# Gate steps of a mixture of experts with operands in a PSUM bank, transposes of two tiles in one bank, scatter places copied out of the rows, and own banks for the last two tiles

## The chip, the cores and the metric

The kernel runs on one core of a Trainium2 chip. The metric is the device time of one execution in microseconds (us). TensorE is called PE here, VectorE DVE, ScalarE ACT, GpSimd POOL and SyncE SP, as in the profile. SBUF is the on-chip memory that all engines read. PSUM is the memory that PE writes its results into; it has banks of 128 x 512 fp32 values ("bank" below always means one of these).

## The reference

Three stages, each feeding the next, in fp32:

```
x = scan(x, a, B, C)                 # state space scan, 4 x 8 x 768 x 32, chunks of 32
x = x.reshape(3072, 256)
h = x @ w_in                         # FFN, 256 -> 2048, rational activation
g = (a0 + a1 h + a2 h^2 + a3 h^3) / (1 + |b0||h| + |b1|h^2 + 1e-6)
x = g @ w_out                        # 2048 -> 256
# mixture of 8 experts, each token to its best one
xn = x / (norm(x) + 1e-6);  en = emb / (norm(emb) + 1e-6)
logits = xn @ en.T / tau
idx = argmax(logits);  p = softmax(logits)     # exp, sum + 1e-9, divide
out[n] = p[n, idx[n]] * (relu(x[n] @ w1[idx[n]]) @ w2[idx[n]])   # 256 -> 1024 -> 256
```

## The kernel before

The whole program is recorded as a list of operations, and a planner (class `Plan`) writes it out in an order of its own. Each operation gives its engine (or a choice of engines), an assumed length, and a number `at`. At each moment a free engine takes, of the operations whose inputs are ready and whose buffers are free, the one with the smallest `at`. Buffers come from groups with a name ("tag") and a fixed count; a group hands them out strictly in the order of their first use. Each engine then runs its own list in that fixed order, and waits where an input isn't there yet.

**The mixture of experts.** A token's row has 265 numbers: 256 values, 8 logits, and its place in the output as an integer. `route` (L778) computes logits of 128 tokens at a time (`tk`, PE L799 and L801; copied to `row` by ACT L804), finds each token's expert, and POOL scatters the rows into an expert's region of `xs` in DRAM. Then passes run over experts sorted by how many tokens they hold.

- Three *first passes* (`first_pass`) take 256 tokens of each of the three largest experts, with fp32 weights `fa`, `fb`; they are interleaved with the end of the FFN, so PE has work while routing finishes. Their rows are `fg`, their first matmuls `fh`, their activations `fr`, their second matmuls `fy`.
- The *later passes* (`run_pass`) take 256 more tokens of each of these three, 384 of each of the four smallest (`e4` to `e7`), and last 512 of expert 3 in two parts. These use weights split into a high and a low half, loaded by `weights` (L935): SP's queue loads `ra` or `rb` (L946), ACT rounds to the high half `eah`/`ebh` (L947), and DVE or POOL subtracts to get the low half `eal`/`ebl` (L950). The four buffers of tag "raw" that receive `ra` and `rb` also hold the rows `fg` of the first passes.

A later pass consists of: `tokens` (L955), which loads rows `g`, transposes them on PE (`t`, L969), and splits the transpose into `xh` (ACT L972) and `xl` (DVE L975); `gate` (L981), which computes the softmax weight `gt` of each token from its own row by some 11 small DVE steps on 128 x 2 to 128 x 32 numbers (L994 to L1008: `s`, `sq`, `rc`, `mx`, `ex`) with ACT steps between (L990, L995, L996, L1005); eight times `hidden` (L1011), with matmuls `eh` (L1023), `hh` on ACT (L1025), `hl` on DVE (L1026) and second matmuls `y` (L1032); and `deliver` (L1038), which scales `y` by `gt` into `yo` (ACT or DVE, L1046 or L1048) and scatters it to the output from POOL (L1052, an indirect DMA whose places are read from the rows `g`).

After all routing, `beyond` (L1176) counts the tokens that fit in no pass: one small matmul `ck` and nine or so small DVE steps.

The FFN's lines are L738 to L755 (`h`, `v`, `u`, `p`, `gh`, `gl`, `acc`); L776 writes its result `x2T`.

Of the kernel before, what the change touches and what calls it, by code (L numbers as in the profile page):

```python
# [275 lines left out]
def ssm_ffn_moe_kernel(  # L276
# [153 lines left out]
    tri, ones = keep([P, P], BF16, "tri"), keep([P, P], BF16, "ones")  # L430
    io, tok, cw8, ke, kmin = keep([P, NE], I32, "io"), keep([P, NCH], I32, "tok"), keep([P, NE], F32, "cw8"), keep([P, NE], BF16, "ke"), keep([P, NE], F32, "kmin")
# [1050 lines left out]
```

## Time and profile before

| | |
|---|---|
| time, median of 3 runs | 608.58 us (608.17 to 608.62) |
| the profiled execution, time | 609.72 us |
| its span in the trace | 607.9 us, granted clock 0.980 in the mean |
| PE busy | 555.0 us, 91% |
| DVE busy | 478.7 us, 79% |
| ACT busy | 467.1 us, 77% |
| POOL busy | 249.7 us, 41% |

The span is the time from the first to the last event of the trace; an execution's time has 1.8 us around it. The chain of waits that ends last goes through PE for 59% of the span. The FFN ends at about 418 us in the span, routing and first passes fill the time to about 457, and the later passes run from there to 595.3; the last 12.6 us deliver the last tiles.

### The profile page before, as it was taken

To read this page: it belongs to the slowest core of one execution; us is meant where nothing else is said; L and a number is where in the kernel's file an instruction comes from. 1 tells how busy PE (TensorE), PEld (TensorE's weight loads), DVE (VectorE), ACT (ScalarE), POOL (GpSimd) and SP (SyncE) were. 2 spreads that over 40 slices of the span, in tenths; PEclk is the share of its full clock that TensorE was granted. 3 is DMA by queue.
4 is the path that set the end of the run, shared out by engine and by line. 5 is a ranking of instruction groups with operands and counts; after the bars stand their busy time and mean duration, and the time that the engine had idled before them with its cause. 6 is when DMAs were issued, how large, how long until landed. Compare 5 with 4: busy or idle time off the path is not lost.

```text
span 607.9 us, 10415 instructions
## 1 busy us (share of the span) xinstructions
PE 555.0 (91%) x3429; PEld 430.0 (71%) x3429; DVE 478.7 (79%) x989; ACT 467.1 (77%) x941; POOL 249.7 (41%) x233
## 2 busy tenths in 40 slices
PE   1667989999999999999999999899998979999991
PEld 0244657776667666767676787677888979999991
DVE  7997899989888798899997889884456667767430
ACT  6898989999998899989997998893256667557330
POOL 2573334446444444454445434433433543222111
PEclk9997999999999999999999999999999989999996
DMA  7960515113102120110010001681266855544000
GB/s 245 390 206 18 160 30 160 45 55 97 45 0 84 51 61 19 54 62 18 2 46 27 1 2 54 219 286 36 89 193 174 238 154 177 173 142 153 18 23 14
DMA packets 47919, 61.08 MB, mean 100 GB/s; under 512 B 4135, under 2 KB 37776, under 8 KB 47856
## 3 DMA queue, kind: packets, MB, share of 16 engines
q1 hardware_dynamic: 45360, 53.92, 29.0%
q0 software_dynamic: 2496, 6.41, 2.9%
q8 instruction: 29, 0.48, 0.4%
q14 instruction: 34, 0.28, 0.1%
HBM read 46.11 MB, written 14.72 MB: 100 GB/s over the span
## 4 chain that ended last, share of the span: by engine, by line
PE 59%; issue 8%; DMA 7%; DVE 7%; ACT 4%; POOL 3%; SPq 1%; another core or an unknown queue 0%; POOLq 0%; ACTq 0%
PE h L738 19%; PE acc L764 19%; PE eh L1023 4%; PE y L1032 4%; PE c L666 3%; DMA g<-xs 2%; PE y L706 2%; PE y L712 2%; DMA ra<-in_w 2%; POOL out_dram L1052 1%; PE tk L801 1%; PE fy L1119 1%; DMA out_dram<-yo,g 1%; DMA fa<-in_w 1%; DVE gh L752 1%
## 5 line engine op out<-in xcount | busy, mean ns | idle before, releaser
L755 POOL TENSOR_TENSOR gl<-p,v 128x512 fp32r<-128x512 f32 x96 | 127.4, 1329 | 176.0 <-DVE p L754 76.1
L738 PE MATMUL h<-x1h,wiw 128*128 128x512 f32 x384 | 142.0, 413 | 7.5 <-DVE p L754 5.2
L764 PE MATMUL acc<-gh,wow 128*128 128x512 f32 x384 | 112.0, 413 | 0.0
L738 PEld LDWEIGHTS h<-x1h,wiw 128*128 128x128 f32 x384 | 73.5, 192 | 34.0 <-issue 7.6
L764 PEld LDWEIGHTS acc<-gh,wow 128*128 128x128 f32 x384 | 68.0, 188 | 29.6 <-issue 15.9
L752 DVE SCALAR_TENSOR_TENSOR gh<-h,as,v 128x512 fp32r<-128x512 f32 x96 | 71.7, 747 | 14.1 <-ACT v L750 13.5
L753 DVE SCALAR_TENSOR_TENSOR u<-u,lq,gh 128x512 f32<-128x512 f32 x96 | 78.9, 822 | 0.8
L747 DVE SCALAR_TENSOR_TENSOR h<-p,sl,h 128x512 f32<-128x512 f32 x96 | 71.9, 749 | 6.7 <-ACT v L744 6.4
L738 PE MATMUL h<-x1l,wiw 128*128 128x512 f32 x192 | 76.8, 400 | 0.0
L743 ACT ACTIVATE p<-h,kk 128x512 f32<-128x512 f32 x96 | 65.3, 680 | 11.8 <-POOL gl L755 6.1
L754 DVE SCALAR_TENSOR_TENSOR p<-h,as,u 128x512 f32<-128x512 f32 x96 | 71.6, 745 | 3.0 <-DVE bw L651 0.2
L745 ACT ACTIVATE u<-v,qb 128x512 f32<-128x512 f32 x96 | 69.5, 724 | 1.5
L749 ACT ACTIVATE v<-u,lq 128x512 f32<-128x512 f32 x96 | 69.4, 722 | 1.6
L750 ACT ACTIVATE v<-v 128x512 f32<-128x512 f32 x96 | 60.4, 630 | 1.0
L764 PE MATMUL acc<-gl,wow 128*128 128x512 f32 x192 | 60.6, 396 | 0.1
L744 ACT ACTIVATE v<-h 128x512 f32<-128x512 f32 x96 | 56.9, 593 | 2.5 <-POOL gl L755 2.5
L1026 DVE SCALAR_TENSOR_TENSOR hl<-eh,hh 128x256 fp32r<-128x256 f32 (+1 forms) x72 | 34.2, 479 | 27.3 <-ACT hh L1025 26.8
L1025 ACT ACTIVATE hh<-eh 128x256 fp32r<-128x256 f32 (+1 forms) x72 | 30.5, 425 | 28.2 <-PE eh L1023 24.4
L1052 POOL DMA_INDIRECT out_dram<-yo,g x22 | 23.8, 1080 | 67.8 <-DVE yo L1048 34.6
L1032 PE MATMUL y<-ebh,hh 128*128 128x256 f32 x176 | 51.2, 291 | 0.3 <-ACT hh L1025 0.3
L1032 PE MATMUL y<-ebh,hl 128*128 128x256 f32 x176 | 50.5, 287 | 0.2 <-DVE hl L1026 0.2
L1032 PE MATMUL y<-ebl,hh 128*128 128x256 f32 x176 | 49.8, 283 | 0.0
(238 smaller groups left out, 1143.1 us busy)
## 6 DMA issues: line engine op xcount, KB each, us to landing
ra<-in_w SPq DMA_DIRECT2D x32, 256.0 KB
rb<-in_w SPq DMA_DIRECT2D x32, 256.0 KB
xb<-in_xb SPq DMA_DIRECT2D x12, 384.0 KB
xs<-empty SPq DMA_DIRECT2D x8, 530.0 KB
wiwr<-in_w_in SPq DMA_DIRECT2D x8, 512.0 KB
wowr<-in_w_out SPq DMA_DIRECT2D x8, 512.0 KB
xrow<-row SPq DMA_DIRECT2D x6, 530.0 KB
bc<-in_bct SPq DMA_DIRECT2D x12, 256.0 KB
```

The costliest lines, as they stand in the source:

```text
L738: T.matmul(out=h.t, lhsT=part(wiw[g_], z)[:, k, fs], rhs=xx[:, k, :], start=(k == 0 and e == 0), stop=(k == 1 and e == 2))
L743: op("ACT", act(512, 1), s, lambda: A.activation(out=pp.t, in_=h.t, func=AF.Square, bias=kk.t), r=[h, kk], w=[pp])
L745: op("ACT", acts(512) + 0.06, s + 0.3, lambda: A.activation(out=uu.t, in_=vv.t, func=AF.Square, bias=qb.t), r=[vv, qb], w=[uu])
L747: op("DVE", dve(512, 1), s + 0.8, lambda: stt(out=h.t, in0=pp.t, scalar=sl.t, in1=h.t, op0=ALU.add, op1=ALU.mult), r=[h, pp, sl], w=[h])
L749: op("ACT", acts(512) + 0.09, s + 0.9, lambda: A.activation(out=vv.t, in_=uu.t, func=AF.Ln, bias=lq.t), r=[uu, lq], w=[vv])
L750: op("ACT", acts(512), s + 1.0, lambda: A.activation(out=vv.t, in_=vv.t, func=AF.Exp, scale=-1.0), r=[vv], w=[vv])
L752: op("DVE", dve(512, 1), s + 1.5, lambda: stt(out=gh.t, in0=h.t, scalar=as_.t, in1=vv.t, op0=ALU.add, op1=ALU.mult), r=[h, as_, vv], w=[gh])
L753: op("DVE", dve(512, 1), s + 1.6, lambda: stt(out=uu.t, in0=uu.t, scalar=lq.t, in1=gh.t.bitcast(F32), op0=ALU.add, op1=ALU.mult), r=[uu, l ...
L754: op("DVE", dve(512, 1), s + 1.7, lambda: stt(out=pp.t, in0=h.t, scalar=as_.t, in1=uu.t, op0=ALU.add, op1=ALU.subtract), r=[h, as_, uu], w ...
L755: op("POOL", pool2(512), s + 2.1, lambda: G.tensor_tensor(out=gl.t, in0=pp.t, in1=vv.t, op=ALU.mult), r=[pp, vv], w=[gl])
L764: T.matmul(out=acc[dh].t, lhsT=part(wow[g_], z)[:, i % 2, dh * P:(dh + 1) * P], rhs=x.t, skip_group_check=True, start=(i == 0 and e == 0), ...
L1032: T.matmul(out=y[t // 2][:, t % 2 * DM:(t % 2 + 1) * DM], lhsT=hx[:, o], rhs=wb[w][:, f % 2, :], start=(f == 0 and i == 0 and t % 2 == 0), ...
```

## The change

1. **Gate's steps with operands in a bank.** All gates but that of the first small pass take a bank (`gp`, of the four with tag "h" that `eh` and `fh` use too) and put `rc`, the later `sq`, `mx` and `ex` there; none of the steps then has two inputs in SBUF. One DVE step (the clamp, L994) is dropped: ACT's Ln gets the constant 1e-36 as its bias from a tile `tiny`, set once on POOL.
2. **Two tiles' transposes to a bank.** `tokens` transposes two tiles into one bank, and one ACT copy and one DVE subtraction of 512 columns do what two of 256 did.
3. **Places copied out of the rows.** POOL copies the places into `ix` (later passes) or `fix` (first passes); the scatter reads them there, and so the rows `g` and `fg` are no longer held until it.
4. **The last two tiles in own banks** (`apart`). In the last part of the last pass each tile's `y` has a bank and its matmuls are an operation of their own; the first tile's `yo` then depends on its own matmuls alone.

```
+    op("POOL", 0.1, 30.0, lambda: G.memset(tiny.t, 1e-36), w=[tiny])
...
-        for t in range(n):
+        for t in range(0, n, 2):
+            m = min(2, n - t)
...
-            op("PE", 0.218, at - 2 + 0.3 * t, f, r=[g, ident], w=[tr])
-            op("ACT", act(256), sh(at - 2 + 0.3 * t, 0.08, 0), f1, r=[tr], w=[(xh, t)])
-            op("DVE", dve(256), at + -2.0 + 0.3 * t, f2, r=[tr, (xh, t)], w=[(xl, t)])
+            op("PE", 0.218 * m, at - 2 + 0.3 * t, f, r=[g, ident], w=[tr])
+            op("ACT", act(256 * m), at - 2 + 0.3 * t + 0.08, f1, r=[tr], w=xp(xh))
+            op("DVE", dve(256 * m), at - 2.0 + 0.3 * t, f2, r=[tr] + xp(xh), w=xp(xl))
...
+        if bankd:
+            gp = plan.val(ps_h, [P, 512], F32, f"gp{nm}", "h", H_B, True)
+            SN, RC, MX, EX = ((gp, k) for k in range(4))
+            sn, rc, mx3 = ((lambda k=k: gp[:, 32 * k:32 * k + n]) for k in range(3))
+            ex = lambda: gp[:, 96:96 + n * NE].rearrange("p (t e) -> p t e", e=NE)
...
-        dv(0.08, lambda: V.tensor_scalar(out=s2[:, 0:n], in0=s2[:, 0:n], scalar1=1e-36, scalar2=None, op0=ALU.max), [s2], [s2])
...
-        dv(0.1, lambda: V.reciprocal(out=rc[:, 0:n], in_=s[:, 0:n]), [s], [rc])
-        dv(0.08, lambda: V.tensor_tensor(out=rc[:, 0:n], in0=rc[:, 0:n], in1=s2[:, 0:n], op=ALU.mult), [rc, s2], [rc])
-        dv(0.08, lambda: V.tensor_tensor(out=s[:, 0:n], in0=s[:, 0:n], in1=rc[:, 0:n], op=ALU.add), [s, rc], [s])
...
+        dv(0.1, lambda: V.reciprocal(out=rc(), in_=s()), [S], [RC])
+        dv(0.08, lambda: V.tensor_tensor(out=rc(), in0=rc(), in1=s2[:, 0:n], op=ALU.mult), [RC, s2], [RC])
+        dv(0.08, lambda: V.tensor_tensor(out=sn(), in0=s(), in1=rc(), op=ALU.add), [S, RC], [SN])
+        dv(0.08, lambda: V.tensor_scalar(out=sn(), in0=sn(), scalar1=0.5, scalar2=1e-6, op0=ALU.mult, op1=ALU.add), [SN], [SN])
+        dv(0.1, lambda: V.reciprocal(out=rs(), in_=sn()), [SN], [RS])
...
+        for t in range(n):
+            op("PE", 1.4 / 4, sh(at + 0.8, 0.36, 0) + (6.0 if t == n - 1 and f > 4 else 0.0), lambda t=t: mm2([t], 1), r=[hh, hl, *wb], w=[y[t]])
...
-            op("POOL", 1.04, sh(at + 0.5 + 0.1 * (t - t0), 3.33, 0), f, r=[yo, g], w=[(out_v, (nm, t))], size=P * DM * 4, port=False)
+            op("POOL", 1.04, sh(at + 0.5 + 0.1 * (t - t0), 3.33, 0), f, r=[yo, ix], w=[(out_v, (nm, t))], size=P * DM * 4, port=False)
...
-        gt = gate(plan, nm, g, sum(parts), at + 2 * parts[0] - 2.0, sp)
+        gt = gate(plan, nm, g, sum(parts), at + 2 * parts[0] - 2.0, sp, True, [tiny])
+        ix = plan.val(sp, [P, TPE], I32, f"ix{nm}", "ix", 4)
+        op("POOL", 0.15, at + 2 * parts[0] - 2.0, lambda n=sum(parts): G.tensor_copy(out=ix[:, 0:n], in_=g[:, 0:n, ROW - 1].bitcast(I32)), r=[g], w=[ix])
...
-        gt = gate(plan, nm, g, n, at + 4 * step, blk)
+        gt = gate(plan, nm, g, n, at + 4 * step, blk, not small, [tiny])
+        ix = plan.val(blk, [P, 2], I32, f"fix{nm}", "fix", 3)
```

The planner then writes another order. DVE, in the pass over the third largest expert, just before the pass over `e4` begins (`hl_2_3` is `hl` of this pass's fourth step, `t_4_0_0` and `xh_0` belong to `e4`). Before:

```order
L1026 SCALAR_TENSOR_TENSOR hl_2_2_5594<-eh_2_2_5552,hh_2_2_5578 128x256
L950 TENSOR_TENSOR eal_0_2_5607<-ra_0_2_5495,eah_0_2_5589 128x512
L1026 SCALAR_TENSOR_TENSOR hl_2_3_5620<-eh_2_3_5582,hh_2_3_5609 128x256
L997 RECIPROCAL rc_0_5626<-sq_0_5596 128x3
L998 TENSOR_TENSOR rc_0_5626<-rc_0_5626,s_0_5534 128x3
L999 TENSOR_TENSOR sq_0_5596<-sq_0_5596,rc_0_5626 128x3
L1000 TENSOR_SCALAR sq_0_5596<-sq_0_5596 128x3
L1001 RECIPROCAL rc_0_5626<-sq_0_5596 128x3
L1026 SCALAR_TENSOR_TENSOR hl_2_4_5647<-eh_2_4_5613,hh_2_4_5635 128x256
L975 TENSOR_TENSOR xl_0_5652<-t_4_0_0_5631,xh_0_5644 128x2x128
L1004 TENSOR_TENSOR ex_0_5538<-ex_0_5538,rc_0_5626 128x24
L975 TENSOR_TENSOR xl_0_5652<-t_4_0_1_5649,xh_0_5644 128x2x128
```

and with the change (line numbers are those of the changed kernel; `gp` is the bank):

```order
L1042 SCALAR_TENSOR_TENSOR hl_2_2_5577<-eh_2_2_5538,hh_2_2_5561 128x256
L952 TENSOR_TENSOR eal_0_2_5587<-ra_0_2_5485,eah_0_2_5572 128x512
L1042 SCALAR_TENSOR_TENSOR hl_2_3_5600<-eh_2_3_5565,hh_2_3_5589 128x256
L952 TENSOR_TENSOR eal_0_3_5606<-ra_0_3_5532,eah_0_3_5591 128x512
L1042 SCALAR_TENSOR_TENSOR hl_2_4_5627<-eh_2_4_5593,hh_2_4_5613 128x256
L1013 RECIPROCAL gp_2_5629<-sq_2_5241 128x2
L980 TENSOR_TENSOR xl_0_5638<-t_4_0_0_5608,xh_0_5625 128x2x256
L1014 TENSOR_TENSOR gp_2_5629<-gp_2_5629,s_2_5217 128x2
L1015 TENSOR_TENSOR gp_2_5629<-sq_2_5241,gp_2_5629 128x2
L1016 TENSOR_SCALAR gp_2_5629<-gp_2_5629 128x2
L1017 RECIPROCAL rc_2_5658<-gp_2_5629 128x2
```

The gate of `e4` (four steps ahead of `hl_2_4` before) has gone from this place; the gate of the running pass stands here instead, and `xl` comes ahead of its multiplications. A low half of weights (`eal_0_3`) that POOL made before now stands on DVE between `hl_2_3` and `hl_2_4`.

ACT at the end of the FFN (`x2T` is the FFN's last result, `row` the routed rows, `eah_2_1` the second high half of weights of the first later pass). Before:

```order
L1005 ACTIVATE ex_0_4475<-ex_0_4475 128x16
L1113 ACTIVATE fr_0_4_4682<-fh_0_4_4672 128x256
L1005 ACTIVATE ex_0_4624<-ex_0_4624 128x16
L947 ACTIVATE ebh_2_0_4685<-rb_2_0_4650 128x512
L1098 ACTIVATE fx_0_4712<-ft_0_4701 128x512
L776 ACTIVATE x2T_4723<-acc_0_4015,fin 128x512
L776 ACTIVATE x2T_4723<-acc_1_4016,fin 128x512
L947 ACTIVATE eah_2_1_4731<-ra_2_1_4708 128x512
L804 ACTIVATE row_3991<-tk_4733 128x264
L804 ACTIVATE row_3991<-tk_4744 128x264
```

and with the change:

```order
L1140 ACTIVATE fr_0_4_4665<-fh_0_4_4659 128x256
L949 ACTIVATE eah_2_1_4687<-ra_2_1_4647 128x512
L1123 ACTIVATE fx_0_4693<-ft_0_4682 128x512
L778 ACTIVATE x2T_4704<-acc_0_4017,fin 128x512
L778 ACTIVATE x2T_4704<-acc_1_4018,fin 128x512
L806 ACTIVATE row_3993<-tk_4712 128x264
L806 ACTIVATE row_3993<-tk_4723 128x264
L949 ACTIVATE ebh_2_1_4738<-rb_2_1_4680 128x512
L806 ACTIVATE row_3993<-tk_4731 128x264
```

`eah_2_1` has moved from between `x2T` and `row` to ahead of `x2T`, and two of the three first passes' exponentials (L1005) are gone from the FFN's end: these gates now stand behind the FFN's end, in the first passes themselves. PE's order is nearly the same; its new pieces are the two tiles' transposes that stand together, and the last pass's `y` in halves. PE has no wait on a bank `gp` that it had not on another.

## Rows read from the trace of the kernel before

**Rows 1.** Busy time by stretch of the span: PE, PEld, DVE, ACT, POOL, clock, DMA.

```profile
core 0: us, PE busy (x) PEld busy (x) DVE busy (x) ACT busy (x) POOL busy (x), PEclk, DMA share, GB/s
...
421.50:428.00 6.50, 5.25 (x26) 4.55 (x25) 0.43 (x1) 1.69 (x4) 0.00 (x0) 0.74 0.00 0
...
455.00:460.00 5.00, 3.64 (x27) 3.11 (x26) 2.46 (x10) 2.87 (x7) 3.47 (x4) 1.00 0.50 141
460.00:490.90 30.90, 30.57 (x249) 29.57 (x248) 21.78 (x54) 21.18 (x55) 13.58 (x12) 1.00 0.67 199
490.90:494.40 3.50, 0.00 (x0) 0.00 (x0) 3.40 (x8) 0.42 (x2) 2.17 (x2) 1.00 0.40 119
494.40:500.50 6.10, 6.09 (x37) 6.09 (x38) 2.73 (x11) 3.37 (x11) 2.52 (x2) 0.72 0.79 235
500.50:595.30 94.80, 94.50 (x707) 93.95 (x705) 58.36 (x145) 51.42 (x135) 20.72 (x19) 1.00 0.36 110
```

**Rows 2.** Timeline of PE: start, us, instruction, [idle before it <- releaser].

```profile
404.25 0.50 PE L738 MATMUL h<-x1h,wiw 128*128 128x512 f32 x1 [0.74 <-DVE p L754]
...
422.77 0.44 PE L799 MATMUL tk<-ident,x2T 128*128 128x128 f32 x2 [1.25 <-ACT row L804]
...
457.72 0.24 PE L1181 MATMUL ck<-oh,ones 128*128 128x8 bf16 x4 [1.36 <-DVE xl L975]
...
494.41 0.44 PE L969 MATMUL t<-ident,g 128*128 128x128 f32 x2 [3.56 <-DVE xl L975]
```

**Rows 3.** Timeline of DVE from 490 to 495.

```profile
490.18 2.93 DVE L998 TENSOR_TENSOR rc<-rc,s 128x3 f32<-128x3 f32 x1
493.14 0.16 DVE L999 TENSOR_TENSOR sq<-sq,rc 128x3 f32<-128x3 f32 x1
...
494.36 0.42 DVE L975 TENSOR_TENSOR xl<-t,xh 128x256 fp32r<-128x256 f32 x1
```

**Rows 4.** Timeline of POOL over the same stretch.

```profile
490.59 1.28 POOL L950 TENSOR_TENSOR eal<-ra,eah 128x512 fp32r<-128x512 f32 x1
491.80 1.27 POOL L950 TENSOR_TENSOR ebl<-rb,ebh 128x512 fp32r<-128x512 f32 x1
```

**Rows 5.** One line at a time: DVE durations, ns min/median/max.

```profile
L998 DVE TENSOR_TENSOR rc<-rc,s x11: 153/163/2927, 403.3 to 554.8; 128x2 f32<-128x2 f32 x6, 128x3 f32<-128x3 f32 x4, 128x4 f32<-128x4 f32 x1
...
L1007 DVE TENSOR_SCALAR gt<-gt x11: 153/165/1680, 409.7 to 559.4; 128x2 f32<-128x2 f32 x6, 128x3 f32<-128x3 f32 x4, 128x4 f32<-128x4 f32 x1
...
L753 DVE SCALAR_TENSOR_TENSOR u<-u,lq,gh x96: 733/747/3703, 52.8 to 414.4; 128x512 f32<-128x512 f32 x96
...
L752 DVE SCALAR_TENSOR_TENSOR gh<-h,as,v x96: 728/748/753, 51.5 to 413.6; 128x512 fp32r<-128x512 f32 x96
```

**Rows 6.** Timeline of ACT around 422.

```profile
421.81 0.63 ACT L947 ACTIVATE eah<-ra 128x512 fp32r<-128x512 f32 x1 [2.48 <-DMA ra<-in_w]
422.35 0.37 ACT L804 ACTIVATE row<-tk 128x264 f32<-128x264 f32 x1
```

**Rows 7.** SP's DMA queue, then POOL, before 419.

```profile
418.73 0.37 SPq L946 DMA_DIRECT2D ra<-in_w  x1
...
417.44 1.27 POOL L950 TENSOR_TENSOR ebl<-rb,ebh 128x512 fp32r<-128x512 f32 x1
```

**Rows 8.** Timeline of ACT around 456.

```profile
455.21 0.63 ACT L947 ACTIVATE eah<-ra 128x512 fp32r<-128x512 f32 x1 [0.85 <-DMA ra<-in_w]
...
456.84 0.64 ACT L972 ACTIVATE xh<-t 128x256 fp32r<-128x256 f32 x2
```

**Rows 9.** Instructions by line, POOL: busy us, mean ns.

```profile
L792 POOL COPY row<-tok 128x4 int32<-128x4 int32 x6 | 2.6, 426 | 0.1
```

**Rows 10.** The end of the program: PE, then DVE.

```profile
594.60 0.28 PE L1032 MATMUL y<-ebh,hl 128*128 128x256 f32 x1
...
594.96 0.28 PE L1032 MATMUL y<-ebh,hl 128*128 128x256 f32 x1
...
595.28 0.88 DVE L1048 TENSOR_SCALAR yo<-y,gt 128x256 f32<-128x256 f32 x2 [1.31 <-PE y L1032]
```

More of the change, by code (lines that the diff above doesn't have):

```diff
@@ L1009, in gate, with hidden @@
         return gt
-    def hidden(nm, e, t0, n, f, xh, xl, y, at):
+    def hidden(nm, e, t0, n, f, xh, xl, y, at, apart=False):
         h = plan.val(ps_h, [P, 512], F32, f"eh{nm}_{f}", "h", H_B, True)
@@ L1026, in hidden, with mm2 @@
         op("DVE", dve(m), sh(at + 0.2, -2.22, 0), lambda: V.scalar_tensor_tensor(out=hl[:, 0:m], in0=h[:, 0:m], scalar=0.0, in1=hh[:, 0:m].bitcast(F32), op0=ALU.max, op1=ALU.subtract), r=[h, hh], w=[hl])
-        def mm2():
-            for t in range(n):
+        def mm2(tiles, per):
+            for t in tiles:
                 o = slice(t * P, (t + 1) * P)
@@ L1032, in mm2, with deliver @@
                     T.matmul(
-                        out=y[t // 2][:, t % 2 * DM:(t % 2 + 1) * DM], lhsT=hx[:, o], rhs=wb[w][:, f % 2, :],
-                        start=(f == 0 and i == 0 and t % 2 == 0), stop=(f == 7 and i == 2), skip_group_check=True,
-                    )
-        op("PE", 1.4 * n / 4, sh(at + 0.8, 0.36, 0), mm2, r=[hh, hl, *wb], w=y)
-    def deliver(nm, t0, n, g, y, gt, at):
+                        out=y[t // per][:, t % per * DM:(t % per + 1) * DM], lhsT=hx[:, o], rhs=wb[w][:, f % 2, :],
+                        start=(f == 0 and i == 0 and t % per == 0), stop=(f == 7 and i == 2), skip_group_check=True,
+                    )
+        if not apart:
+            op("PE", 1.4 * n / 4, sh(at + 0.8, 0.36, 0), lambda: mm2(range(n), 2), r=[hh, hl, *wb], w=y)
+            return
+        for t in range(n):
+            op("PE", 1.4 / 4, sh(at + 0.8, 0.36, 0) + (6.0 if t == n - 1 and f > 4 else 0.0), lambda t=t: mm2([t], 1), r=[hh, hl, *wb], w=[y[t]])
+    def deliver(nm, t0, n, ix, y, gt, at, per=2):
         for t in range(t0, t0 + n):
             yo = plan.val(w3, [P, DM], F32, f"yo{nm}_{t}", "yo", 4)
-            b = (t - t0) // 2
-            src = lambda t=t, b=b: y[b][:, t % 2 * DM:(t % 2 + 1) * DM]
+            b = (t - t0) // per
+            src = lambda t=t, b=b: y[b][:, (t - t0) % per * DM:((t - t0) % per + 1) * DM]
             def f(eng, t=t, yo=yo, src=src):
@@ L1066, in run_pass @@
             nm = f"{e}_{t0 + q}"
-            y = [plan.val(*z, True) for z in [(ps_a, [P, 512], F32, f"y{nm}_{b}", "acc", 2) for b in range((n + 1) // 2)]]
+            per = 1 if apart and q + n == sum(parts) else 2
+            y = [plan.val(*z, True) for z in [(ps_a, [P, 512], F32, f"y{nm}_{b}", "acc", 2) for b in range((n + per - 1) // per)]]
             for f in range(8):
-                hidden(nm, e, q, n, f, xh, xl, y, at + f * n / 4)
+                hidden(nm, e, q, n, f, xh, xl, y, at + f * n / 4, per == 1)
             at += 2 * n
-            deliver(nm, q, n, g, y, gt, at + 0.9)
+            deliver(nm, q, n, ix, y, gt, at + 0.9, per)
             q += n
```

54 lines of the change are left out of this document (30 added, 24 removed).

## The prediction, made before the changed kernel was run

> **What bounds the kernel now.** I read the busy time by stretch first, to see which engine the end follows. From 500.5 to 595.3 PE is busy 94.50 of 94.8 us and DVE 58.36; from 460 to 490.9 PE 30.57 of 30.9 and DVE 21.78 [rows 1]. So PE is the bound of the whole mixture, and a saving on DVE, ACT, POOL or a queue is worth only what it takes out of PE's idle time. I then went through PE's timeline for the places where it stands still. Four are worth naming: 0.74 us at 404 behind DVE's `p`; 1.25 at 422.77, where the transposes `tk` wait for ACT's `row`; 1.36 at 457.72, where `ck` waits for `xl`; and 3.56 at 494.41, where the transposes of `e4` wait for `xl` [rows 2]. Two of them cost more than they last: the stretch from 421.5 to 428 has a granted clock of 0.74 in the mean, that from 494.4 to 500.5 of 0.72, between stretches at 1.00 [rows 1], and PE had idled just before or within them. By these rows the lost clock is (1 - 0.74) x 6.5 = 1.69 us and (1 - 0.72) x 6.1 = 1.71 us.
>
> The reader should next ask why DVE is late at 494. Its timeline shows that `xl` itself is short (0.42); ahead of it the multiplication `rc<-rc,s` on 128 x 3 numbers took 2.93 us, up to 493.11 [rows 3]. The same line takes 0.163 us in the median [rows 5]. POOL ran two 128 x 512 subtractions with both inputs in SBUF in that time, from 490.59 to 491.87 and on to 493.07 [rows 4]. The multiplication ends when they end. Across the program DVE lines with two SBUF inputs are stretched now and then (L998 up to 2927 ns, L753 up to 3703 against 747), while L752, of the same size but with one operand in a bank, lies between 728 and 753 in all its 96 executions [rows 5]. L1007, a step with one SBUF input and a constant, is stretched too (1680).
>
> **The change part by part.** *Gate in a bank.* The multiplication and addition get one operand from a bank, L1007's step is in a bank altogether, one DVE step per gate goes. What the stall at 490 costs today is 3.56 of idle and 1.71 of clock, 5.27 us. No row shows a 128 x 3 step on a bank, so its length is bounded from both sides: nothing saved if it is stretched as before, all 5.27 if it behaves as L752. I take 5.1, near L752's end, since that row is the same engine, beside the same POOL work, with just this operand placement; and the order shown above also moves the gate of `e4` out of the place and `xl` ahead of the running gate's multiplications, which protects `xl` even if they are slow.
>
> The Trainium skill says the same from the other side ("SBUF — State Buffer", section "Who interferes with whom"): a DVE instruction with two SBUF inputs shares a port pair with a GpSimd instruction that reads SBUF, whoever has it first keeps it for the whole instruction, and one with at most one SBUF input, outside DVE's two-port modes, does not contend. The trace agrees as far as it goes (released at 493.11, POOL's pair done at 493.07). By this rule the gate's part is worth the full 5.27; but it also speaks against the change elsewhere, since the new POOL copies read SBUF, and `eal_0_3`, now on DVE with two SBUF inputs ahead of `hl_2_4`, stays exposed: that is the second rival below.
>
> *Gates moved off the FFN's end.* Two of three first-pass gates leave DVE at 402 to 416. The wait of 0.74 at 404 [rows 2] may go wholly or stay (the first gate is still there, unbanked). I take 0.5 of 0 to 0.74.
>
> *Rows released sooner, loads earlier.* At 422 ACT stood for 2.48 us at `eah`, whose load had just been issued, and `row`, queued behind it, came at 422.35 [rows 6]; PE waited for `row`. The load was issued at 418.73, just after POOL's `ebl` of 417.44 (1.27 long) freed its raw buffer [rows 7]. By the code, three of the four raw buffers were held by `fg` until their scatters. With the places copied out, the first `fg` is free after its gate, so two buffers circulate instead of one: `ra_2_1` now follows the first subtraction and not the second, and lands before ACT's list comes to `eah_2_1`, which now stands ahead of `x2T`. Worth 0 (the load is as late as before, and then `x2T` waits behind it) to 1.25 + 1.69 = 2.94. I take 2.7. The same holds at 455, where ACT waited 0.85 for `ra` before `eah`, in front of `xh` at 456.84 [rows 8], and PE's 1.36 follow from that. Between 0 and 1.36 I take the 0.85 of that one wait.
>
> *Two tiles in a bank.* ACT's two 256-column copies took 0.64 together [rows 8], one 512-column copy takes 0.63 [rows 6]; on DVE two of 0.42 [rows 3] become one of 0.75 (L752, the 512-column row [rows 5]). Nothing is saved where PE doesn't wait, and `xl` of the first tile is 0.3 later. I take 0; the cover is PE's next `eh`/`y` work, and without it the cost is 0.3 in each of eight places, 2.4 in the worst case, at the edge of the range.
>
> *Places copied out.* Eleven POOL copies of 128 x 2 to 4 numbers; the nearest row is 0.43 us each (L792) [rows 9], 4.7 in all. POOL is idle for over half of the stretch from 460 on (13.58 busy of 30.9, 20.72 of 94.8 [rows 1]), so I take 0. Queued behind a copy that waits for `g` are low halves of weights, which PE needs a pass later.
>
> *Own banks at the end.* DVE's `yo` at 595.28 waited for the last matmul, which began at 594.96; the first tile's last one began at 594.60 [rows 10]. The first `yo` and its scatter can start 0.36 earlier. POOL's two scatters then follow each other, so the end moves by 0.36; I take that, of 0 to 0.36.
>
> *What is late next.* The reorder leaves DVE instructions with two SBUF inputs in new places (`eal` in front of `hl_2_4`, `beyond`'s steps in front of the first `hl`). I charge one stall of one POOL subtraction, 1.27 [rows 4], between 0 and twice that.
>
> **Sum.** 5.1 + 0.5 + 2.7 + 0.85 + 0.36 - 1.27 = 8.24. From the profiled execution's 609.72 us that leaves 601.5. That execution was 1.14 above the median of the runs (608.58), so I forecast 608.58 - 8.24, rounded to 600.3.
>
> **The rivals.**
> 1. *Only the stall at 490 goes.* The loads are limited by something else (DMA, or the two later `fg`, now held until later gates), and 422 and 457 stay: 5.1 + 0.36 - 1.27 = 4.2, 604.4 us. For it: at 455, over 30 us later, ACT still waits for a load [rows 8]. Against: ACT at 422 waited for one load only, and its issue follows a freed buffer.
> 2. *The stall moves.* `eal_0_3` or `beyond`'s steps meet POOL's subtractions, `hl` is late by 2.5 to 3 us and PE idles as before, with the clock loss; or a bank operand doesn't help. The 5.1 is gone, the rest stays: 8.24 - 5.1 = 3.1, 605.4 us. For it: L753 has been held for 3703 ns. Against: the planner keeps the low halves of DVE and POOL apart, and PE has work queued between `eh` and `y`.
> 3. *Slower: the bank held by a gate starves `eh`.* Ten gates take one of four banks through their whole chain, with ACT steps between. If each makes PE wait w us, the time is above 608.58 from w = 0.83 on, and by w = 1.1 it is 611.3. Against: a hidden step occupies a bank for its six matmuls, one `hh` and one `hl` only, and three banks remain; no `eh` waits on a `gp` in the order written.
> 4. *The change does nothing*: gains of 404, 422 and 457 don't come, and rival 2 too: 608.6 or so.
>
> **How the numbers follow.** Forecast 0.62 (its own range 597.5 to 602.5: all bounds at their best give 5.27 + 0.74 + 2.94 + 1.36 + 0.36 = 10.67, 597.9, with some small gaps not listed); rival 1 0.16; rival 2 0.12; rival 3 0.05; rival 4 0.05. The range from 597.4 to 605.0 takes in the forecast, rival 1, and the better half of rival 2, 0.84 in all, the excess being for what I haven't seen. A measurement can tell about 0.2% here, 1.2 us: faster is below 607.4, which forecast, rivals 1 and 2 are: 0.90, and I say 0.88; the same 0.06; slower 0.06.
>
> **What would show it right or wrong.** Right: no gate step on DVE above 0.3 us but in the first gate; PE's timeline without the gaps at 422, 457 and 494; clock at 1.00 in their neighbourhood; ACT's `eah_2_1` with no wait for its load. Wrong: gaps of over 1 us in PE that end with `hl` or `eh`, DVE's `eal` or `on` rows above 1 us, ACT's `x2T` behind a wait for `ra`, or PE waiting for a bank that a gate holds.

## The result, and the profile of the changed kernel

The changed kernel takes 593.4 us in the median of four runs (592.5 to 594.2) against 608.6 for the kernel before: ratio 0.9756, 95% interval 0.9715 to 0.9797. Run again on two other chips it gave 0.9766 (0.9722 to 0.9809) and 0.9788 (0.9758 to 0.9818). So the change gives some 2.3%, 13 to 15 us, where I forecast 8.2 us; the time lies below my range. Its profiled execution took 593.66 us, with a span of 592.0.

The busy time by stretch, which answers to [rows 1]:

```profile
core 0: us, PE busy (x) PEld busy (x) DVE busy (x) ACT busy (x) POOL busy (x), PEclk, DMA share, GB/s
395.00:417.00 22.00, 20.24 (x93) 16.80 (x92) 15.35 (x29) 17.71 (x40) 9.35 (x8) 1.00 0.55 174
421.50:428.00 6.50, 6.50 (x39) 5.70 (x39) 3.05 (x11) 0.88 (x3) 1.26 (x1) 1.00 0.44 121
455.00:460.00 5.00, 5.00 (x45) 5.00 (x44) 3.66 (x13) 3.79 (x8) 3.36 (x4) 1.00 0.78 226
460.00:490.90 30.90, 30.90 (x253) 30.90 (x252) 22.11 (x64) 24.65 (x71) 17.55 (x18) 1.00 0.78 224
490.90:500.00 9.10, 9.10 (x67) 9.10 (x67) 6.31 (x13) 5.46 (x13) 3.46 (x3) 1.00 0.56 178
500.00:579.50 79.50, 79.50 (x600) 79.39 (x599) 49.95 (x133) 41.53 (x106) 16.12 (x17) 1.00 0.34 101
```

PE is now busy without a break from 421.5 to the end of its work, at a clock of 1.00. What it still waits for from 378 on is all before that (who waited for whom: us in total, times, longest):

```profile
PE h L740 <- DVE p L756: 2.3, 2, 1.3
PE h L740 <- ACT fr L1140: 1.8, 1, 1.8
PE acc L766 <- POOL gl L757: 0.2, 1, 0.2
```

None of the four gaps of [rows 2] is left in its place, but near the one at 404 a new one has come, at 398.50: PE waits for `fr` of ACT, and ACT had stood for the rows of a first pass at `jk` (a gate's squares of a row). PE, then ACT:

```profile
398.50 0.50 PE L740 MATMUL h<-x1h,wiw 128*128 128x512 f32 x1 [1.76 <-ACT fr L1140]
...
392.67 0.42 ACT L1006 ACTIVATE jk<-fg 128x256 f32<-128x256 f32 x1 [2.46 <-DMA fg<-xs]
```

At the FFN's end the load is issued at 408.67, 4.5 us before `eah` starts, which doesn't wait for it (its 2.73 us are for a first pass's matmuls `fh`, which still read the buffer that `eah` takes over), and `row` follows `tk` at once; compare [rows 6] and [rows 7]. SP's queue, then ACT:

```profile
408.67 0.37 SPq L948 DMA_DIRECT2D ra<-in_w  x1
415.18 0.37 SPq L948 DMA_DIRECT2D rb<-in_w  x1
...
413.16 0.63 ACT L949 ACTIVATE eah<-ra 128x512 fp32r<-128x512 f32 x1 [2.73 <-PE fh L1136]
...
418.15 0.39 ACT L806 ACTIVATE row<-tk 128x264 f32<-128x264 f32 x1 [1.26 <-PE tk L803]
```

Where DVE stood for 2.93 us in [rows 3], `xl` of `e4` now comes 0.5 us after `hl`, and the gate's multiplication behind it takes 0.16. No gate step takes more than 199 ns anywhere. First DVE's timeline there, then two steps by line (ns min/median/max), against [rows 5]:

```profile
481.80 0.43 DVE L1042 SCALAR_TENSOR_TENSOR hl<-eh,hh 128x256 fp32r<-128x256 f32 x1
482.14 0.16 DVE L1013 RECIPROCAL gp<-sq 128x2 f32<-128x2 f32 x1
482.29 0.69 DVE L980 TENSOR_TENSOR xl<-t,xh 128x512 fp32r<-128x512 f32 x1
482.90 0.16 DVE L1014 TENSOR_TENSOR gp<-gp,s 128x2 f32<-128x2 f32 x1
```

```profile
L1014 DVE TENSOR_TENSOR gp<-gp,s x10: 157/169/170, 433.2 to 564.6; 128x2 f32<-128x2 f32 x5, 128x3 f32<-128x3 f32 x4, 128x4 f32<-128x4 f32 x1
...
L1020 DVE TENSOR_TENSOR gp<-gp,rc x10: 176/182/199, 436.2 to 566.2; 128x16 f32<-128x16 f32 x5, 128x24 f32<-128x24 f32 x4, 128x32 f32<-128x32 f32 x1
```

The end, which answers to [rows 10] (PE, DVE, ACT, POOL): the first `yo` starts before PE's last matmul, and POOL's scatters start 0.36 us sooner after it.

```profile
581.21 0.28 PE L1048 MATMUL y<-ebh,hl 128*128 128x256 f32 x1
...
581.17 0.48 DVE L1069 TENSOR_SCALAR yo<-y,gt 128x256 f32<-128x256 f32 x1 [0.95 <-PE y L1048]
...
581.52 0.47 ACT L1067 ACTIVATE yo<-y,gt 128x256 f32<-128x256 f32 x1 [1.77 <-PE y L1048]
...
581.93 0.97 POOL L1073 DMA_INDIRECT out_dram<-yo,ix  x1 [6.95 <-DVE yo L1069]
```

**Five stretches.** Executions of one kernel differ: the kernel before took 600.45 to 607.73 us on one chip, so a difference of a few us between two traces is not yet the kernel's. I therefore cut each trace at the same instructions of PE, which stand in the same order in all of these kernels but for a few pieces: the counting matmul `cn` in the FFN (372.48 in the trace of before), the first `tk` (419.83), the first transposes of the later passes (454.02), the first 384-column `eh` of `e4` (499.77), the last `y` (594.96), and the span's end. Differences of start times, us:

| kernel | cn to tk | tk to t | t to e4 | e4 to last y | to the end | from cn |
|---|---|---|---|---|---|---|
| before | 47.35 | 34.19 | 45.75 | 95.19 | 12.97 | 235.4 |
| control (before again) | 47.58 | 33.15 | 45.91 | 95.26 | 13.03 | 234.9 |
| changed | 48.26 | 31.06 | 37.70 | 95.06 | 10.76 | 222.8 |
| after_again | 47.78 | 31.06 | 37.70 | 95.06 | 10.77 | 222.4 |
| after_third | 47.67 | 31.06 | 37.70 | 95.05 | 10.89 | 222.4 |
| no_bank | 50.48 | 32.38 | 43.38 | 95.50 | 10.79 | 232.5 |
| no_places | 48.98 | 32.40 | 42.48 | 95.77 | 10.80 | 230.4 |
| no_pairs | 47.92 | 31.06 | 38.03 | 95.10 | 10.78 | 222.9 |
| no_apart | 47.43 | 31.06 | 37.71 | 95.05 | 12.85 | 224.1 |
| bank_only | 49.24 | 32.39 | 43.96 | 95.09 | 11.13 | 231.8 |
| places_only | 50.19 | 32.27 | 41.47 | 94.87 | 12.59 | 231.4 |
| apart_only | 47.13 | 32.47 | 43.45 | 95.64 | 10.80 | 229.5 |
| bank_places | 47.47 | 31.07 | 38.23 | 95.10 | 11.13 | 223.0 |
| raw5 | 48.50 | 31.07 | 41.29 | 98.85 | 12.97 | 232.7 |
| same_order | 47.35 | 31.06 | 38.95 | 95.05 | 10.80 | 223.2 |
| late_fg | 47.73 | 34.99 | 37.72 | 95.05 | 10.77 | 226.3 |
| late_fg8 | 47.15 | 31.06 | 37.71 | 95.05 | 10.83 | 221.8 |
| bank_late8 | 47.30 | 31.06 | 45.83 | 95.46 | 11.13 | 230.8 |

From `cn` on, the two traces of the kernel before take 235 us and the three of the changed kernel 222 to 223: 12.1 to 13.0 us are the program's. The other 3.35 us of the two profiles' 15.96 stand ahead of `cn`, where PE's order is the same in all of these kernels. Part of them is the change's all the same (last section).

A wait costs PE somewhat more than the idle time that its row shows: matmuls of 256 columns follow each other every 0.12 us (three steps from 594.60 to 594.96 in [rows 10]), but each is listed with 0.28, so from start to start at least 0.16 us more is lost.

### The profile page after: what moved, and what is told of

Same layout as the page of the kernel before. It is cut to its first block, busy times and chain, and to the rows that moved or that the text cites. A ratio compares the mean times of both kernels' runs of the same rounds, so it can differ in the third digit from the quotient of the medians.

```text
span 592.0 us, 10406 instructions
## 1 busy us (share of the span) xinstructions
PE 546.0 (92%) x3429; PEld 428.0 (72%) x3429; DVE 472.0 (80%) x967; ACT 466.9 (79%) x933; POOL 253.6 (43%) x246
## 4 chain that ended last, share of the span: by engine, by line
PE 71%; ACT 8%; issue 5%; DVE 4%; DMA 1%; POOL 1%; SPq 1%; POOLq 0%; ACTq 0%; DVEq 0%
PE acc L766 18%; PE h L740 18%; PE eh L1039 9%; PE y L1048 9%; PE fy L1146 3%; PE fh L1136 3%; PE c L668 3%; PE y L708 2%; ACT p L745 2%; PE y L714 1%; ACT u L747 1%; PE tk L803 1%; DMA fg<-xs 1%; ACT v L751 1%; PE st L690 1%
## 5 line engine op out<-in xcount | busy, mean ns | idle before, releaser
L752 ACT ACTIVATE v<-v 128x512 f32<-128x512 f32 x96 | 60.5, 630 | 1.0
L1073 POOL DMA_INDIRECT out_dram<-yo,ix x22 | 23.1, 1050 | 53.5 <-DVE yo L1069 37.6
```

The source lines that it names most:

```text
L752: op("ACT", acts(512), s + 1.0, lambda: A.activation(out=vv.t, in_=vv.t, func=AF.Exp, scale=-1.0), r=[vv], w=[vv])
```

## The experiments

Ratios are to the kernel before on the same chip, with 95% intervals; runs that are compared most closely shared a chip.

**The kernel before once more** (control; no edit).

> The kernel before, unchanged, profiled once more. The changed kernel's trace is ahead of that of before by 3.75 us at 363 us of its span already, where PE's, DVE's and ACT's orders are still the same. Theory one: that lead comes with the execution or the chip and not with the change; then this trace reaches the first matmul of the FFN's last tiles 2 to 4 us before the trace of before did, or the lead of the changed kernel over it at that point is under 1 us. Theory two: the change brings it (where its buffers lie, say); then the lead over this trace is 3 to 4 us again. The time is that of before by either, within 0.2%.

Ratio 1.0007 (0.9975 to 1.0039). `cn` starts at 368.15 us, 4.3 sooner than in the trace of before and 1.0 sooner than in the changed kernel's. By the two leads theory one holds: most of what separates two traces ahead of `cn` belongs to the execution. It doesn't hold whole: PE's pace there differs between kernels, in the same way on every chip (last section). The trace shows a second thing: behind the same gap at `tk` (1.31 us here, 1.25 before) PE's clock stays at 1.00 (second fence, busy time from 421 to 428), where it fell to 0.74 in the mean in [rows 1]. My 1.69 us there were of that one execution.

```profile
418.73 0.44 PE L799 MATMUL tk<-ident,x2T 128*128 128x128 f32 x2 [1.31 <-ACT row L804]
```

```profile
421.00:428.00 7.00, 7.00 (x42) 6.14 (x42) 3.05 (x11) 1.18 (x4) 1.26 (x1) 1.00 0.35 115
```

**Without one part each** (no_bank, no_places, no_pairs, no_apart: the changed kernel with one part undone).

```
no_bank    gate(plan, nm, ..., sp, False, [tiny])       # and False in first_pass
no_places  ap=ix[:, t:t + 1]  ->  ap=g[:, t, ROW - 1:].bitcast(I32)    # no ix, no fix
no_pairs   for t in range(0, n, 1):  m = 1
no_apart   run_pass(e, t0, parts, at)
```

> The changed kernel, but every gate keeps its steps in SBUF (the dropped clamp, the pairs of transposes, the copied places and the last own banks stay). Theory one, the two-input steps are what POOL's subtractions hold up: DVE has gate steps of 0.6 to 3 us again, at least one of them makes PE wait with a loss of clock, and the time is 596 to 600 us. Rival, the stall at 490 went because the planner put the gate elsewhere: no more than 594.6 us, and no PE gap above 1 us behind the FFN.

Ratio 0.9905 (0.9871 to 0.9940): within theory one's time, but not for its reason. DVE's gate steps are held up again (ten above 0.3 us, up to 1.98), yet no single stall as at 490 is back. The order is another one, and the loss is spread: 5.7 us from `t` to `e4`, seven waits of 0.2 to 1.0 among it, for `fr`, `xl` and `hl`; 1.1 at `tk`; and 2.2 to 2.8 from `cn` to `tk`, where DVE's `mx` of a first pass stands in the FFN and waits for rows that haven't landed, `fr` behind it, and PE behind `fr`. Behind this wait the clock falls, to 0.72 in the mean of 6 us, which by these figures is 1.7 us of the 2.2 to 2.8. DVE, then PE, then the busy time by stretch:

```profile
390.49 0.17 DVE L1018 TENSOR_REDUCE mx<-fg 128x2 f32<-128x16 f32 x1 [2.61 <-DMA fg<-xs]
...
392.10 0.41 DVE L1142 TENSOR_SCALAR fr<-fh 128x256 f32<-128x256 f32 x1
...
392.57 0.50 PE L740 MATMUL h<-x1h,wiw 128*128 128x512 f32 x1 [2.23 <-DVE fr L1142]
...
392.00:398.00 6.00, 5.43 (x17) 4.31 (x18) 5.00 (x14) 5.35 (x13) 2.42 (x2) 0.72 1.10 346
```

> The changed kernel, but the scatter reads the places from the rows again, which stay held until it. Theory one, the rows' buffers made the weights late: ACT waits for ra around 420 again, PE has the gap before tk with the loss of clock and one before ck, and the time is 596.5 to 598.5 us (593.4 plus 2.7 to 3.6, and up to 1.5 more). Rival, the deferred gates and the merged transposes did that: no more than 594.6 us.

Ratio 1.0006 (0.9973 to 1.0039): nothing of the gain is left, more than theory one said. Its profile fell on its fastest execution (600.39 us of 600.39 to 608.58), and even there PE loses 8 us from `cn` on. What I had named as the danger, under *Rows released sooner, loads earlier*, is here: ACT's `eah`, now ahead of `x2T`, waits 4.75 us for its load, and `tk` waits for `x2T`. With the fall of the clock behind it (0.81 in the mean from 417 to 426) that makes some 2 of the 8 us; 4.8 more go from `t` to `e4`, most of it in two waits: 1.64 for `fr`, queued on ACT behind weights whose loads are late again, and 1.08 for `xl`.

```profile
415.98 0.63 ACT L949 ACTIVATE eah<-ra 128x512 fp32r<-128x512 f32 x1 [4.75 <-DMA ra<-in_w]
416.52 1.25 ACT L778 ACTIVATE x2T<-acc,fin 128x512 f32<-128x512 f32 x2
...
417.24 0.33 PE L801 MATMUL tk<-ident,x2T 128*128 128x128 f32 x1 [1.77 <-ACT x2T L778]
```

> The changed kernel with tiles transposed one by one. Theory one, the pairs are worth nothing: 211.6 to 212.1 us from cn to PE's last matmul, within 0.25% of the changed kernel. Rival, they save DVE and ACT a step where PE waits for xl: 0.5 to 1 us more between the first transposes of the later passes and the first 384-column matmul (37.7 in the changed kernel, 38.2 with neither pairs nor own banks).

Ratio 0.9808 (0.9785 to 0.9832), beside 0.9774 for no_apart on the same chip. In the trace the pairs are worth 0.33 us (38.03 against 37.70), but the profile fell on the fastest of the five runs (591.88 of 591.88 to 596.24). In the medians no_pairs is 2.0 us above no_apart, which has no own banks in turn; the intervals leave room for 0.33 and for some 4 us. What the pairs are worth stays open between these.

> The changed kernel with the last two tiles in one bank. By theory one it loses 0.36 us. By theory two the scatter lands 0.36 later and then meets the instruction packet or misses it as it falls: 11.1 us from the last matmul to the end, or 12.5 to 13. All else as in the changed kernel: 211.6 to 212.1 us from cn to the last matmul.

Ratio 0.9774 (0.9749 to 0.9798). In this trace the end takes 12.85 us, 2.1 more than with own banks: theory two, the case in which the packets meet.

**One part alone, and two** (bank_only, places_only, apart_only, bank_places: the changed kernel with the other parts undone by the same edits). The clamp stays dropped in all, and no run drops it alone.

> Of the change only the gate: its steps in a bank and the clamp dropped. Places are read from the rows, tiles are transposed one by one, the last tiles share a bank. Theory one, the stall at 490 is worth 5.1 us and belongs to this part: 608.6 - 5.1 = 603.5 us, 602 to 605, with the gap at 422 still there. Rival, a bank operand doesn't help: 607.4 us or more.

Ratio 0.9961 (0.9927 to 0.9996). DVE's gate steps are short, and the wait at `t` is 0.86 us in place of 2.90. But `eah` stands ahead of `x2T` as in no_places, and PE waits 2.06 for `x2T`. The part alone gives 2.4 us, not 5.1: neither theory. Of the 3.1 us that its trace is ahead of the control from `cn` on, 1.9 stand behind the last `y` (11.13 against 13.03), where this kernel has no own banks (more on that in the last section).

```profile
418.65 0.33 PE L801 MATMUL tk<-ident,x2T 128*128 128x128 f32 x1 [2.06 <-ACT x2T L778]
...
491.17 0.44 PE L974 MATMUL t<-ident,g 128*128 128x128 f32 x2 [0.86 <-DVE xl L980]
```

> Of the change only the copied places (and the dropped clamp): gates stay in SBUF. Theory one: the rows' buffers come free, the gap before tk goes, DVE's gate steps are held up as in the control (some 10 us above their medians): ratio 0.990 to 0.996. Rival, the two parts pay only together, since a held-up gate keeps its rows and thereby the buffer: 0.998 or more.

Ratio 0.9906 (0.9871 to 0.9942): in theory one's range. Ten gate steps on DVE take above 0.3 us, 11.3 in all, as it says; but the gap before `tk` doesn't go. PE waits 0.99 there for `row`, now queued behind an `eah` that waits not for its load but for a first pass's `fy`. It also waits 2.35 for `fr` in the FFN and 1.15 for `xl` at `e4`.

> Of the change only the own banks of the last two tiles (and the gate without its clamp). Theory one, it moves the last scatter up by 0.36 us and no more: from PE's last matmul to the span's end 12.6 us against 13.0 in the control. Theory two: the scatter then also lands ahead of a 16 KB packet of the instruction queue that it stood behind in before and in the control: 10.8 us, 2.2 less, ratio 0.995 to 0.998 with all else as in the control (gaps before tk, ck and t, held-up gate steps).

Ratio 0.9937 (0.9914 to 0.9960), better than either theory. The end takes 10.80 us as theory two says; but this kernel's order is not that of before, since the clamp is gone and the gates' steps stand elsewhere: PE's wait at `t` is 1.81 us instead of 2.9 with no clock drop behind it (one does follow the wait of 1.92 at `ck`: 0.76 in the mean from 453 to 460). From `cn` to the last `y` it is 3.2 us ahead of the control, with none of the other parts in it: that must be laid to the dropped clamp and the order that the planner then writes.

> Gate in a bank and places copied out; tiles transposed one by one, and the last tiles share a bank. Theory one, these two parts carry the change: within 0.3% of the changed kernel in this call, with 0.36 us less at the end. Rival, the merged transposes keep xl from being late at the starts of passes: PE waits for xl or t by over 1 us in all, and the time is 0.5% or more above the changed kernel.

Ratio 0.9785 (0.9742 to 0.9828), beside 0.9766 for the changed kernel on the same chip. Theory one: bank and places carry the change. Alone they take 3.1 and 3.5 us off the stretches from `cn` (control 234.9), together 11.9. Without the end, which differs by chance in kernels with no own banks, it is 1.2, 3.1 and 10.0 up to the last `y`, beside 3.2 for apart_only, which has neither part. So in these traces, next to a kernel that only lacks the clamp there, the bank alone shows no gain and the places alone none either; the two together show some 7 us.

> The changed kernel again, beside the runs of before that the other kernels of this call share. If the changed kernel's lead of 3.75 us before the FFN's end was of the execution and not of the change (as the control says, which had 4.35 over the trace of before), then PE's part from the last counting matmuls of the FFN (cn) to its last matmul is 212 us again, 10 us less than in the control (221.9), the tail gives some 2 us more, and the ratio is 0.978 to 0.982. If the change earned the lead as well, the ratio is below 0.976.

Ratio 0.9766, 211.60 us from `cn` to the last `y`, 10.77 to the end: from `cn` on it is as the first theory says; the ratio lies between the two figures and is too wide to say more. For the lead ahead of `cn` see the last section.

**Five raw buffers** (the kernel before, `raw` with 5 buffers, `yo` with 2).

> The kernel before with five buffers of tag raw in place of four (and two of yo in place of four, to make room), nothing else. Theory one, the gap before tk is a raw buffer that comes free late: eah_2_1 finds its load landed, PE has no gap above 0.4 us at the tk matmuls, and of the change's gain the 2.9 of that place and about 0.9 at the next come: ratio 0.992 to 0.995; DVE's gate steps are still held up (several above 0.5 us). Rival, the weights' DMAs themselves are the limit: the gaps before tk and ck stay within 0.3 us of the control's 1.3, ratio 0.999 or more.

Ratio 0.9962 (0.9930 to 0.9994). The gap at `tk` is gone (`tk` to `t` 31.07, as in the changed kernel), with no place copied out: theory one, though the ratio lies above its range. `yo`'s two buffers cost 3.6 us from `e4` on, which the ratio holds too.

**The changed kernel's order, gate steps in SBUF** (same_order). The planner still reckons with the bank, so that every engine's list is the same, word for word but for the tile's name; the steps' numbers lie in a tile of the scan.

```
-            sn, rc, mx3 = ((lambda k=k: gp[:, 32 * k:32 * k + n]) for k in range(3))
+            sn, rc, mx3 = ((lambda k=k: mask[:, z + 4 * k:z + 4 * k + n]) for k in range(3))
...
-            ex = lambda: gp[:, 96:96 + n * NE].rearrange("p (t e) -> p t e", e=NE)
+            ex = lambda: mask[:, z + 12:z + 12 + n * NE].rearrange("p (t e) -> p t e", e=NE)
```

> The changed kernel, in its own order on every engine, but the gates' steps that it keeps in a bank lie in SBUF (in the mask tile of the scan, which is not used any more by then). Theory one, the operands' place is what counts: DVE's gate steps are held up again by POOL's subtractions (several above 0.5 us, some 8 to 11 us in all above their medians), PE waits for hl or xl at some of them, and the time is 0.4 to 1.0% above the changed kernel. Rival, the gain came from the order: DVE's steps are long, but PE has no new wait above 0.3 us, and the time is within 0.2% of the changed kernel.

Ratio 0.9818 (0.9788 to 0.9847), the changed kernel beside it 0.9788 (0.9758 to 0.9818); medians 592.05 and 590.52 us. The outcome lies between the two theories. DVE's steps are held up again: eight above 0.3 us, 6.9 us in all (5.5 above their medians), where the changed kernel has none. PE loses 1.25 us by it, from `t` to `e4`, and nothing in any later stretch; `cn` to `tk` is 0.3 shorter than in after_third. The multiplications by line, then PE's new waits, which from start to start are 1.1 of the 1.25:

```profile
L1017 DVE TENSOR_TENSOR mask<-mask,s x10: 149/164/1506, 429.2 to 561.8; 128x2 f32<-128x2 f32 x5, 128x3 f32<-128x3 f32 x4, 128x4 f32<-128x4 f32 x1
...
L1023 DVE TENSOR_TENSOR mask<-mask,rc x10: 168/174/1206, 432.1 to 563.5; 128x16 f32<-128x16 f32 x5, 128x24 f32<-128x24 f32 x4, 128x32 f32<-128x32 f32 x1
```

```profile
447.24 0.38 PE L1042 MATMUL eh<-xh,eah 128*128 128x256 f32 x1 [0.26 <-ACT xh L978]
...
447.96 0.39 PE L1042 MATMUL eh<-xl,eah 128*128 128x256 f32 x1 [0.34 <-DVE xl L981]
```

So in the new order the operands' place does count, and is worth 1.25 us in the traces and 1.5 in the medians, of 13. no_bank, which lets the planner write an order for gates in SBUF, loses 10 us from `cn` on; the rest of the bank's part is therefore the order. By the code that is the planner's doing, which now lets a gate begin only when it has a bank to give. The stall at 490 itself shrinks in every other order, also with the steps in SBUF: PE's wait at this `t` is 2.90 in the control, none in no_bank and here, and in raw5, places_only and apart_only:

```profile
489.82 0.44 PE L969 MATMUL t<-ident,g 128*128 128x128 f32 x2 [0.59 <-DVE xl L975]
...
489.33 0.44 PE L974 MATMUL t<-ident,g 128*128 128x128 f32 x2 [1.15 <-DVE xl L980]
...
488.64 0.33 PE L974 MATMUL t<-ident,g 128*128 128x128 f32 x1 [1.81 <-DVE xl L980]
```

What no run shows is the other half, the old order with the steps in a bank: there the operands' place alone might have removed the whole stall.

**Rows reckoned late** (late_fg: the changed kernel with four times the bytes, as in the cut; late_fg8: eight times; bank_late8: eight times, on bank_only).

```
-  ... r=[xs_v, xs_c, one, ranked], w=[g], size=n * P * ROW * 4)
+  ... r=[xs_v, xs_c, one, ranked], w=[g], size=4 * n * P * ROW * 4)
```

> The changed kernel, but the planner reckons the load of the first passes' rows at four times its bytes, so that it puts the gates' steps that read them later. In the changed kernel ACT's jk and DVE's mx stand in their lists before the rows have landed (waits of 1.94 and 0.94 us), with the FFN's steps queued behind them, and PE waits 1.3 to 1.8 us at 397 and up to 1.5 at 386. Theory: these waits go, 1 to 2.5 us less from cn to PE's last matmul, ratio 0.2 to 0.4% below the changed kernel's. Rival: PE's waits there come from DVE's u that is held up for 3 us at 376, and nothing moves: within 0.1%.

Ratio 0.9815 (0.9781 to 0.9850). PE's wait for `fr` goes and the last one for `p` shrinks to 0.64, but `x2T` waits behind `eah` again: PE loses 1.98 us before `tk`, and behind it the clock falls; from `tk` to `t` that is 3.9 us. Neither theory.

> The changed kernel, with the load of the first passes' rows reckoned at eight times its bytes: gates' steps that read them come later, and x2T stands ahead of eah. With four times the waits for the rows went but x2T waited 2 us behind eah. Theory: now both go, 2 us less than the changed kernel from cn to the first tk, ratio 0.2 to 0.4% below it. Rival: weights come later for the first later pass, and PE waits for eah or eal there as much.

Ratio 0.9782 (0.9750 to 0.9813), no difference from 0.9788 that can be told. `x2T` doesn't wait and the gap at `fr` is gone, but one of 1.03 us at `fh` takes its place; the trace is 0.6 us better.

> Bank alone (as before: places from the rows, tiles one by one, last tiles in one bank), but the planner reckons the load of the first passes' rows at eight times its bytes, which puts x2T ahead of eah_2_0 and eah_2_1 on ACT. Theory, the late load of eah_2_1 ahead of x2T ate the bank's gain: PE's wait of 2 us before the first tk goes, and the ratio falls from 0.996 to 0.990 to 0.994; a wait of row behind eah may come in its place. Rival: the weights are late in any order as long as the rows hold the buffers, and the loss moves to row or to the first eh: 0.995 or more.

Ratio 0.9968 (0.9946 to 0.9990): the rival. `tk` waits no more, but the loss moves on: PE waits 2.66 us for `fr` behind ACT's late weights, and the stretch to `e4` is as long as in the control. In the three orders tried with rows that hold the buffers (bank_only, no_places, bank_late8) the wait was only moved.

```profile
450.87 1.13 PE L1144 MATMUL fy<-fb,fr 128*128 128x256 f32 x4 [2.66 <-ACT fr L1138]
...
453.70 0.25 PE L1206 MATMUL ck<-oh,ones 128*128 128x8 bf16 x4 [1.70 <-DVE xl L980]
```

> The changed kernel beside these three: 0.975 to 0.979 by the runs so far, 212 us from cn to PE's last matmul.

Ratio 0.9788; 211.48 us from `cn` to the last `y`.

## Why the prediction was wrong

The step that failed is the sum: three of its terms had the wrong size. The end was bounded at 0.36 us and gave 2.2; a new stall was charged at 1.27 and none came; the stretch around 457 and 490 was taken at 5.95 and gave 8.1 to 8.2. And of the largest term, the 5.1 for the operands' place, the runs show 1.25 in the new order; what else that stretch gained came with the new order and, by raw5, with the buffers that the copied places free.

Term by term, the first figure is the difference between the traces of before and of the changed kernel, the second that between control and after_again.

- **The stall at 490 and the gap at 457** (5.1 and 0.85 forecast, 5.95 together): 8.05 and 8.21 us, the stretch from `t` to `e4`. All that I had listed there is 1.36 + 3.56 + 1.71 = 6.63, of which I took less for 457; 0.33 of idle from 460 to 490.9 [rows 1] is another part. Of the last 1.1 us some 0.6 is what these gaps cost from start to start above the idle that is listed; the other 0.5 is spread over the stretch in pieces too short to be listed.
- **The cause of the stall.** My sentence took "5.1, near L752's end" for the operands' place and named the moved gate as an addition. In the new order same_order shows the sizes the other way round. For the old order no run tells the two apart: either alone may have been enough there, so that the 5.1 comes near the stretch's gain is no proof of its reason. The rule of the Trainium skill that I weighed ("SBUF — State Buffer", section "Who interferes with whom": with at most one SBUF input, outside DVE's two-port modes, a step doesn't contend) agrees with the traces: with its steps in a bank no gate step took over 199 ns in the changed kernel, and with two SBUF inputs, in the same order, up to 1506. Steps with one SBUF input and a constant are held up too (L1007, 1680 ns in [rows 5]); no run shows in which mode these ran. A held-up step costs time only where PE is waiting for what stands behind it; from the one row where that was so I priced them all.
- **The load at 422** (2.7): 3.13 and 2.09. The mechanism was right, as raw5, no_places and the SP row show; the size depends on whether the clock falls behind the gap, which it did in one trace of two.
- **The wait at 404** (0.5): a loss of 0.9 and 0.2. It went, but a new one of 1.8 us came at 398.50, `fr` on ACT behind `jk`, which stands too early in the list for its rows. With the rows reckoned later (late_fg, late_fg8) that wait goes.
- **The end** (0.36, "of 0 to 0.36"): 2.21 and 2.26. This bound was wrong. The scatter starts 0.36 sooner, and by its times that took it out of the way of an instruction packet (below). The other 1.9 us are chance in part: three of the eight traces without own banks miss the packet too.
- **The new stall** (-1.27): none. One `eal` on DVE was held up, to 1.30 us at 433.92, but PE didn't wait for what stood behind it.

So the range missed by three mis-sized terms: the end by 1.9 us, the stall that didn't come by 1.3, and the stretch around 457 and 490 by 2.1 to 2.3; 404 takes about 1 back. From `cn` on that makes the 12.6 of the table (235.4 to 222.8; 234.9 to 222.4 is 12.5). Of the 15.2 between the medians some 2 us may be PE's pace ahead of `cn` (last section), for which the sum had no term; the rest is open: the ratio of the third chip, 0.9788, is 12.9 us of 608.6, and the intervals are wide enough to hold either.

Of the rivals, what the first (422 and 457 stay) and the fourth (no gain) forecast is seen only where a part was undone, as in no_places; the second (the stall moves) and the third (a gate's bank starves `eh`) are not seen in the changed kernel: behind 398.50 PE has no listed wait at all.

**Why the parts pay only together.** Bank and places alone gave 0.4% and 0.9%, together 2.2%; own banks alone gave 0.6%, and all of these hold the dropped clamp. With the bank alone `eah` stands ahead of `x2T` and its load is late; an order that has it behind only moves the wait (bank_only, bank_late8). With the places alone the load is there, but gates' steps that read the first passes' rows still stand in the FFN, and their waits for those rows hold the FFN's steps (places_only, no_bank). So, as I read the waits, each part takes one of two on the same path; the other remains, or grows.

## What to carry to other kernels

Price an instruction that is held up by what PE waits for behind it, not by its own excess: here eight held-up DVE steps, 6.9 us long, cost 1.25. When an edit lets a planner write a new order, test the edit with the order held fixed; otherwise its effect and the order's can't be told apart. And hold the old order fixed as well as the new: that run is missing here. And before bounding the end of a program by the last engine's start, look at what else is in flight on the DMA engines at that moment.

## What the hardware showed that I had not expected

**The last scatter behind an instruction packet.** From the issue of the last scatter to its landing the control takes 4.0 us (first row: line, form, count, us to landing). The second row tells of a later window, 593.9 to 596 (queue, packets, MB, share of the DMA engines):

```profile
out_dram<-yo,g POOLq DMA_INDIRECT x1, 4.0
```

```profile
q8 instruction: 1, 0.02, 3.5%
```

The changed kernel takes 2.2 (after_third):

```profile
out_dram<-yo,ix POOLq DMA_INDIRECT x1, 2.2
```

In the control one 16 KB packet of the instruction queue starts 4.16 us after the last matmul's start and ends at 5.33. Of the scatter queue's 96 packets from then on 93 have ended by 4.1; the other three start at 5.31 to 5.33. With own banks for the last tiles all of them have ended by 3.77 us in ten traces, and the instruction packet starts at 3.84 to 5.10: they don't meet. In the eight traces without own banks they end at 4.1 if nothing is in the way, and the packet starts at 3.75 to 4.80: in five of them (before, control, raw5, places_only, no_apart) three packets are late and the end takes 12.6 to 13.0 us, in the other three 11.1. That the packet causes it is read from these times; no run moved it by itself, and in the control its listed start, 4.16, is already behind the 4.1 by which the three would have ended.

**The clock.** Behind gaps of 1.31 and 2.90 us in the control the clock fell only after the second (0.74 in the mean from 489.4 to 496), while in the trace of before it fell after both 1.25 and 3.56 [rows 1]: the same gap costs 1.7 us in one execution and nothing in the next.

**Speed before any difference.** `cn`, ahead of which PE's order is the same in all 18 traces, starts between 366.06 and 372.48 us. Part of it is PE's pace: between 110 and 367 us two FFN matmuls of 512 columns follow each other in 232 ns in the median in the trace of before (mean 243) and in 230 in that of the changed kernel (mean 240), at the same granted clock of 1.00. That is not the execution's: the median is 230 in each of the eleven traces of kernels with copied places, and 232 in each of the seven without (before, control, raw5, no_places, bank_only, apart_only, bank_late8), on each of the four chips that ran both. The FFN's matmuls of 512 columns, from the 101st to the last ahead of `cn`, take 285.1 to 287.3 us with copied places and 287.6 to 290.8 without, some 2.4 less in the mean, of which a wait right before `cn` takes 0.5 back. So the copied places bring some 2 us that the five stretches leave out and that the sum had no term for. By the code they add two small tiles (`ix`, `fix`) to groups that other buffers share; that this moves where the FFN's buffers lie, and that the pace comes from there, is a guess that no run here tests.
